# Attention then two gated products on one core: where float64 weight conversion starts, in buffers of its own, and the order of the first transfers

## The chip, the cores and the metric

The kernel runs on one core of a Trainium2 chip, with 32-bit float data at full accuracy. The metric is device time in microseconds (us) of one execution; lower is better. TensorE (PE) multiplies matrices, VectorE (DVE), ScalarE (ACT) and GpSimd (POOL) work on tiles, SyncE (SP) issues nearly all transfers. Each engine runs its own instructions strictly in the order in which they stand, so an instruction that waits holds everything behind it.

## The reference

```
h = phi(q), phi(k):  phi(x) = exp(x@omega.T - |x|^2/2 - max) / sqrt(128), x scaled by 64**-0.25
attn = (phi(q) @ (phi(k).T @ v)) / (phi(q) @ sum(phi(k)) + 1e-6)    # 4 batches, 8 heads, 576 x 64
x  = attn as 2304 tokens x 512
g  = silu(x @ w_in);                      x = g @ w_out       # 512 -> 2048 -> 512
g  = silu(x @ w_gate) * (x @ w_val);      out = g @ w_out2    # 512 -> 1536 -> 512
```

The weights reach the chip as float64 words (512 x 2048 and 512 x 1536, and back) and are turned into float32 there.

## The kernel before

**Stages.** Attention runs 72 steps of 128 tokens (8 units of two batch-and-head pairs, 9 steps each). Then follow up 1 (products with w_in), down 1 (w_out), up 2 (w_gate, w_val) and down 2 (w_out2). Every matrix product is done by Strassen's scheme with seven products of half size (numbered 1 to 7, in the order 1, 5, 6, 2, 7, 3, 4 for the down stages), and every float32 operand is split into a rounded high part (made by ACT or POOL) and a low part (the rest, made by DVE or POOL); a product takes high x high, high x low and low x high, so three matmuls.

**Attention.** `load_piece` brings 384 columns of k or q, `split_piece` splits them, `proj` multiplies them by omega (`om_hi`, `om_lo`), `soft` takes the row maximum on DVE (`reduce_max`, L805) and the exponentials on ACT (L809), `kv_tr` and `num` form the sums, `recip`, `spread`, `finish` and `store` divide and write x to DRAM (`x_d`). Working tiles come from `f_work`: nine places in the big tile `fa` and one tile `extra`. Steps are written out in fixed order.

**Up 1.** 24 groups `n` of seven products (8 weight blocks by 3 token ranges s, 384 + 384 tokens each); the first three blocks run over s = 0, then 1, then 2. `x_prep` loads and splits x for one s (into tiles `ra`, `rb`, `rc` for s = 0, 1, 2). After each group four results go to DRAM (`g_d`), 96 in all. Copies between accumulator banks are ACT's (L1160), sums DVE's (L1217), silu ACT's (L1184).

**Conversion.** `conv_job` turns one block of float64 words into float32: two loads (512 KB each), per half a Prelu on ACT (L343), a shift (L350) and an or (L357) on DVE, four sums on POOL (L376), then either a split for up 1 (`conv_job("in", i)`) or three stores of 0.9 MB for a later stage (`down_job`). Blocks in 0, 1, 2 and down 0 are converted during attention, the rest (list `jobs`) in up 1. They use `f_raw` (two load buffers at R_AT), `f_c` and `f_sum`.

**What sets the order.** For the later stages a planner writes instructions as it walks through the products: each operation has an engine, an estimated cost and the keys it needs; `flush` emits what its clocks say is ready, from `urgent` and the streams z, wd, split, x, conv. The down stage's weight loads (stream wd, L1315, split at L1319 and L1323), its first inputs (stream z, L1341, only when the conv stream is empty) and their splits (L1367 on ACT, L1371 and the Strassen sums L1391 on DVE) share the queues with up 1.

**Where conversion starts in up 1.** x for s = 1 is loaded partly into the raw buffers' place (`xr1`), and six places of conversion's buffers are lent to `f_s` (result tiles). So `hook1` starts the conversion only when that x is split and all lent places are back:

```python
def hook1(n, p):
    if conv_may and len(f_s.gone) == len(lent):
        conv_may.clear()
        streams["conv"].extend(conv1)
```

Of the kernel before, what the change touches and what calls it, by code (L numbers as in the profile page):

```python
# [9 lines left out]
F32 = mybir.dt.float32  # L10
# [32 lines left out]
def kernel(  # L43
# [21 lines left out]
    UB = 2  # L65
# [46 lines left out]
    class Free:  # L112
        def __init__(self, name, items):
            self.name = name
            self.q = deque((x, 0.0) for x in items)
            self.retire, self.gone = [], []

        def close(self, some):

            self.retire = some  # L120
            self.gone += [x for x, _ in self.q if any(x is y for y in some)]
            self.q = deque(y for y in self.q if not any(y[0] is z for z in some))
# [534 lines left out]
    def xr1(j, c):  # L657
        return cut(fa, (XR_AT, R_AT)[j] + c * N, N)
# [44 lines left out]
    f_work.give(vp.tile([P, S], F32, name="extra"), 0.0)  # L703
# [12 lines left out]
    CW = UT // 3  # L716

# [13 lines left out]
    def load_v(u):  # L731
        v = v_t[u % 2]
        half = NCH // 2
        for b in range(UB):
            B, p = u_of(u, b)
            for h in range(2):
# [4 lines left out]
                nc.sync.dma_start(out=v[:, c0 : c0 + half, o : o + D], in_=whole)  # L741
                part = src[:D] if b else src[half * P :]
                nc.sync.dma_start(out=v[b * D : (b + 1) * D, half, o : o + D], in_=part)
# [14 lines left out]
    nc.vector.memset(om, 0.0)  # L758
    for h in range(2):
        nc.sync.dma_start(out=om[h * D : (h + 1) * D, h * M : (h + 1) * M], in_=omT)  # L760
    warm = const.tile([P, 1], F32, name="warm")
    nc.gpsimd.memset(warm, 0.0)
    nc.scalar.activation(warm, warm, AF.Exp)
    for i in range(3):
        for nm in ("k", "q"):
            load_piece(0, nm, i)
# [3 lines left out]
    load_v(0)  # L770
# [170 lines left out]
    later, left_over, lent = {}, [], []  # L941
# [4 lines left out]
    for nm, i in pieces:  # L946
        split_piece(0, nm, i)
    for nm, i in pieces:
        load_piece(1, nm, i)
# [4 lines left out]
    def step(s):  # L954
# [34 lines left out]
        if s < NSTEP:  # L989
            if u + 1 < NU and c == LAG:  # L990
                load_v(u + 1)
# [37 lines left out]
    def end_attention():  # L1029
# [12 lines left out]
        lent.extend(cut(fa, o + i * N, N) for o, n in ((C_AT + S // 3, 3), (SUM_AT, 2), (R_AT + 4 * N, 1)) for i in range(n))  # L1042
        for x in lent:
            f_s.give(x, 0.0)

        def rest(ub, n):
# [10 lines left out]
            def after_store(end):  # L1057
                T["xd", B, p] = end + 0.5
                waits.remove(ub)
                if ub[0] == NU - 2 and not any(u == NU - 2 for u, _ in waits):  # L1060
                    f_c.give(c_slot, end)
                    f_s.close(lent)
                    while shut:
                        f_s.give(shut.pop(), end)
# [471 lines left out]
    def up_order(kinds, n, head, tail):  # L1536
# [8 lines left out]
        lambda: x_prep(0, 1, xr1, False, "DVE", then=lambda t: conv_may.append(t)),  # L1545
# [9 lines left out]
    opened, conv_may = [], []  # L1555
# [31 lines left out]

    def hook1(n, p):
        if conv_may and len(f_s.gone) == len(lent):
            conv_may.clear()  # L1590
# [124 lines left out]
```

## Time and profile before

| | |
|---|---|
| three runs | 943.35, 946.96, 947.23 us; median 946.96 |
| the profiled execution | 950.47 us, span 948.7 us |
| busy share of the span | PE 96%, DVE 70%, ACT 60%, POOL 23% |
| stages | attention to about 168 us, up 1 to 352, down 1 to 541, up 2 to 809, down 2 to the end |

A row of a timeline gives the start, the duration, engine, line, operation, output and input, and in brackets how long the engine was idle before it and what ended that. Rows of SPq are the issue of transfers, not the transfers.

### The profile page before, as it was taken

Reading aid. Unit: us, or ns where it says so; the run is one execution under the profiler, and the core shown is the slowest. Engines: PE = TensorE matmul, PEld = TensorE weight load, DVE = VectorE, ACT = ScalarE, POOL = GpSimd, SP = SyncE. Lnnn points to the kernel's source line nnn. Section 1 sums busy time; section 2 is a strip of 40 time slices with the busy share of each in tenths; the row PEclk is TensorE's granted clock in tenths of the full one; section 3 lists DMA queues with packets and bytes.
Section 4 is the critical chain, followed back from the end, with each engine's and each line's share of the span. In section 5 each row is a group of like instructions: output and inputs, shape, how many; then the busy total and the mean of one; then the engine's idle time right before and its main releaser. Section 6 shows DMA issues by size and latency. Waiting matters only on the chain.

```text
span 948.7 us, 15565 instructions
## 1 busy us (share of the span) xinstructions
PE 909.3 (96%) x5313; PEld 883.0 (93%) x5313; DVE 660.6 (70%) x1041; ACT 567.9 (60%) x1231; POOL 214.0 (23%) x258
## 2 busy tenths in 40 slices
PE   7888889999999998999999899999999999899998
PEld 7877778899999997999999799999999999899998
DVE  4667778778575459678589889765647456968594
ACT  6766777677666775545446685544545437545453
POOL 6566885013444200000000012421212110000000
PEclk9989999999999998999999999999999999999999
DMA  6756763688989995551731556643535249472701
GB/s 172 188 159 177 222 178 85 190 274 281 306 288 309 336 392 216 159 175 50 232 119 56 196 165 200 214 157 131 171 112 176 75 138 334 134 207 69 238 20 67
DMA packets 129856, 174.80 MB, mean 184 GB/s; under 512 B 34288, under 2 KB 111728, under 8 KB 129776
## 3 DMA queue, kind: packets, MB, share of 16 engines
q1 hardware_dynamic: 129776, 173.80, 57.6%
q8 instruction: 42, 0.69, 0.3%
q14 instruction: 38, 0.31, 0.1%
HBM read 111.74 MB, written 61.94 MB: 183 GB/s over the span
## 4 chain that ended last, share of the span: by engine, by line
PE 77%; DMA 8%; DVE 6%; ACT 5%; issue 2%; SPq 1%; POOL 0%; DVEq 0%; ACTq 0%
PE ps L1143 39%; PE ps L1508 29%; PE ps L881 2%; ACT kq L809 2%; DMA g_d<-fa 2%; PE ps L829 2%; DMA dn<-fa 2%; DVE nb L805 1%; PE ps L795 1%; PE ps L796 1%; PE ps L797 1%; PE ps L843 1%; DMA fa<-x_d 1%; DMA rc<-wd_out 1%; DMA fa<-g_d 1%
## 5 line engine op out<-in xcount | busy, mean ns | idle before, releaser
L376 POOL TENSOR_TENSOR fa<-fa 128x256 f32<-128x256 f32 x136 | 113.2, 845 | 505.0 <-DVE fa L357 276.9
L1143 PE MATMUL ps<-ra 128*128 128x384 f32 x840 | 156.0, 335 | 3.5 <-ACT ps L1160 3.5
L1143 PE MATMUL ps<-rb,ra 128*128 128x384 f32 x840 | 157.5, 340 | 0.7 <-ACT ps L1160 0.7
L1143 PE MATMUL ps<-rc,ra 128*128 128x384 f32 x840 | 156.6, 339 | 0.1
L1143 PEld LDWEIGHTS ps<-ra 128*128 128x128 f32 x840 | 146.7, 188 | 5.1 <-ACT ps L1160 5.1
L1143 PEld LDWEIGHTS ps<-rb,ra 128*128 128x128 f32 x840 | 148.6, 188 | 1.6 <-ACT ps L1160 1.6
L1143 PEld LDWEIGHTS ps<-rc,ra 128*128 128x128 f32 x840 | 148.3, 188 | 0.4 <-ACT ps L1160 0.4
L1371 DVE TENSOR_TENSOR ra<-fa,ra 128x768 fp32r<-128x768 f32 x105 | 100.5, 957 | 51.9 <-PE ps L1508 30.5
L1367 ACT ACTIVATE ra<-fa 128x768 fp32r<-128x768 f32 x105 | 88.0, 845 | 81.2 <-PE ps L1508 69.2
L1160 ACT ACTIVATE ps<-ps 128x384 f32<-128x384 f32 x180 | 85.3, 475 | 82.6 <-PE ps L1143 77.9
L1217 DVE TENSOR_TENSOR fa<-fa,ps 128x384 f32<-128x384 f32 x120 | 66.2, 552 | 92.4 <-ACT ps L1160 71.5
L1508 PE MATMUL ps<-ra,rb 128*128 128x384 f32 x720 | 129.2, 340 | 0.0
L1508 PEld LDWEIGHTS ps<-ra,rb 128*128 128x128 f32 x720 | 127.9, 189 | 0.5 <-DVE ra L1371 0.3
L1508 PE MATMUL ps<-ra 128*128 128x384 f32 x612 | 110.8, 339 | 6.9 <-DVE ra L1371 6.7
L1508 PEld LDWEIGHTS ps<-ra 128*128 128x128 f32 x612 | 107.3, 190 | 9.4 <-DVE ra L1371 8.5
L809 ACT ACTIVATE kq<-ps,nb 128x128 f32<-128x128 f32 x288 | 82.2, 381 | 40.5 <-DVE nb L805 40.3
L1508 PE MATMUL ps<-ra,rc 128*128 128x384 f32 x432 | 78.5, 340 | 2.5 <-DVE ra L1371 2.5
L1508 PEld LDWEIGHTS ps<-ra,rc 128*128 128x128 f32 x432 | 76.0, 188 | 4.1 <-DVE ra L1371 3.9
L1391 DVE TENSOR_TENSOR fa<-ra,fa 128x768 f32<-128x768 f32 x63 | 60.1, 954 | 1.4 <-DMA ra<-g_d 0.7
L805 DVE TENSOR_REDUCE nb<-ps 128x4 f32<-128x512 f32 x72 | 49.0, 684 | 16.6 <-PE ps L797 11.6
L1184 ACT ACTIVATE fa<-fa 128x384 f32<-128x384 f32 x84 | 43.8, 521 | 27.1 <-DVE fa L1217 26.8
L829 PE MATMUL ps<-v,kq 128*128 128x65 f32 (+1 forms) x320 | 44.8, 279 | 12.8 <-ACT kq L809 8.4
(100 smaller groups left out, 1232.0 us busy)
## 6 DMA issues: line engine op xcount, KB each, us to landing
g_d<-fa SPq DMA_DIRECT2D x168, 192.0 KB, 3.7
fa<-g_d SPq DMA_DIRECT2D x42, 384.0 KB, 4.3
ra<-g_d SPq DMA_DIRECT2D x42, 384.0 KB, 4.0
fa<-in_moe_w_out SPq DMA_DIRECT2D x28, 512.0 KB, 5.2
fa<-in_moe_w_in SPq DMA_DIRECT2D x16, 512.0 KB, 5.4
wd_out<-fa SPq DMA_DIRECT2D x14, 512.0 KB, 3.3
fa<-in_moe_w_gate SPq DMA_DIRECT2D x12, 512.0 KB, 3.8
fa<-in_moe_w_val SPq DMA_DIRECT2D x12, 512.0 KB, 5.6
```

The lines of the kernel that those rows point to most:

```text
L376: f(blk(f"S{n}"), blk(l), blk(r))
L805: nc.vector.reduce_max(nb, ps.rearrange("p i (h m) -> p (i h) m", h=2), axis=AX.X, negate=True)
L809: nc.scalar.activation(e[:, i, h * M : (h + 1) * M], ps[:, i, h * M : (h + 1) * M], AF.Exp, bias=nb[:, 2 * i + h : 2 * i + h + 1],)
L829: nc.tensor.matmul(acc[:, o : o + VH], e[a:z, 0, h * M : (h + 1) * M], vs[u][a:z, c, o : o + VH], start=first and h == 0, stop=last, skip_ ...
L1143: nc.tensor.matmul(ps[b][:, :N], cut(l, j * P, P), cut(r, j * N, N), start=start and c == 0, stop=stop and c == 5, skip_group_check=True,)
L1160: nc.scalar.activation(out() if callable(out) else out, src, AF.Copy)
L1184: nc.scalar.activation(b["t"], src, AF.Silu)
L1217: nc.vector.tensor_add(t, t if in_place else p5[n], ps[bank_][:, :N])
L1367: nc.scalar.activation(ops[s, p, k][0], src(), AF.Copy)
L1371: nc.vector.tensor_sub(l, src(), h.bitcast(F32))
L1391: (nc.gpsimd if eng == "POOL" else nc.vector).tensor_sub(z(PLACE[to]), z(PLACE.get(l, l)), z(PLACE.get(r, r)))
L1508: nc.tensor.matmul(ps[BANKS[p] + e][:, :N], cut(a, e * P, P), b, start=p in FIRST and i == 0 and c == 0, stop=p in LAST and i == fp - 1 an ...
```

## The change

Four edits belong together. (1) x for s = 1 gets a tile of its own (`xr1_t`) beside the v tiles; attention gets four extra working tiles in place of one, and unit NU-2 takes them first, so that conversion's third buffer (`c_slot`) is free when attention's loop ends; nothing is lent. (2) `hook1` starts the conversion stream at n = 0, product 1 (`CONV_P`). (3) `jobs` has down 1 and down 2 first, then in i and down i. (4) The start of attention: k's first piece is loaded before omega, q's first after it, the first half of v on ACT's queue, the other pieces and the rest of v later; only the first pieces are split ahead of the loop; omega is scaled and split on DVE alone; seven matmuls of zeros stand first on PE.

```diff
-        return cut(fa, (XR_AT, R_AT)[j] + c * N, N)
+        return cut(xr1_t, c * N, N) if j else xr(j, c)
...
+        if u == NU - 2:
+            f_work.q = deque(sorted(f_work.q, key=lambda y: any(y[0] is w for w in works)))
...
-    f_work.give(vp.tile([P, S], F32, name="extra"), 0.0)
+    for i in range(4):
+        f_work.give(vp.tile([P, S], F32, name=f"extra{i}"), 0.0)
+    xr1_t = vp.tile([P, 4 * N], F32, name="xr1")
...
-    nc.vector.memset(om, 0.0)
+    zero = const.tile([P, M], F32, name="zero")
+    nc.vector.memset(zero, 0.0)
+    load_piece(0, "k", 0)
     for h in range(2):
         nc.sync.dma_start(out=om[h * D : (h + 1) * D, h * M : (h + 1) * M], in_=omT)
+    load_piece(0, "q", 0)
+    load_v(0, 0, nc.scalar)
...
-    for i in range(3):
+    for i in range(1, 3):
         for nm in ("k", "q"):
             load_piece(0, nm, i)
-    load_v(0)
+    load_v(0, 1)
+    for i in range(WARM):
+        nc.tensor.matmul(ps[0][:, :M], zero, zero, start=True, stop=True)
...
-    nc.vector.tensor_scalar_mul(om, om, SCALE)
-    nc.scalar.activation(om_hi, om, AF.Copy)
-    nc.vector.tensor_sub(om_lo, om, om_hi.bitcast(F32))
+    nc.vector.tensor_scalar_mul(om_hi, om, SCALE)
+    nc.vector.scalar_tensor_tensor(om_lo, om, SCALE, om_hi.bitcast(F32), op0=ALU.mult, op1=ALU.subtract)
...
-    for nm, i in pieces:
-        split_piece(0, nm, i)
-    for nm, i in pieces:
-        load_piece(1, nm, i)
+    for nm in ("k", "q"):
+        split_piece(0, nm, 0)
...
+        if 0 <= s < 2:
+            for nm in ("k", "q"):
+                split_piece(0, nm, s + 1)
+        if s == 1:
+            for nm, i in pieces:
+                load_piece(1, nm, i)
...
-        lent.extend(cut(fa, o + i * N, N) for o, n in ((C_AT + S // 3, 3), (SUM_AT, 2), (R_AT + 4 * N, 1)) for i in range(n))
-        for x in lent:
-            f_s.give(x, 0.0)
+        assert all(o + S <= C_AT for o in taken)
+        f_c.give(c_slot, 0.0)
...
-    jobs = [down_job(0, 1)]
+    jobs = [down_job(0, 1), down_job(0, 2)]
     for i in range(3, FP[0]):
-        jobs += [conv_job("in", i)] + [down_job(0, i - 1)]
-    jobs.append(down_job(0, FP[0] - 1))
+        jobs += [conv_job("in", i), down_job(0, i)]
...
-        if conv_may and len(f_s.gone) == len(lent):
-            conv_may.clear()
+        if n == 0 and p == CONV_P:
             streams["conv"].extend(conv1)
```

PE's row of instructions is the same in both but for the seven matmuls of zeros. Three places where the others change follow; line numbers differ by a few between the two files.

DVE at the start of attention, before (om is cut from `fa`; lok and loq are low parts of k and q, nb the maxima of a step):

```order
L758 MEMSET fa 128x256
L768 MEMSET v_98 128x9
L769 MEMSET v_98 128x9
L768 MEMSET v_99 128x9
L769 MEMSET v_99 128x9
L782 TENSOR_SCALAR fa<-fa 128x256
L784 TENSOR_TENSOR om_lo<-fa,om_hi 128x256
L753 TENSOR_TENSOR lok<-rawk,hik 128x384
L753 TENSOR_TENSOR loq<-rawq,hiq 128x384
L753 TENSOR_TENSOR lok<-rawk,hik 128x384
L753 TENSOR_TENSOR loq<-rawq,hiq 128x384
L805 TENSOR_REDUCE nb<-ps_78 128x4
```

and now:

```order
L754 MEMSET zero 128x128
L761 MEMSET fa 64x128 x2
L766 MEMSET v_102 128x9
L767 MEMSET v_102 128x9
L766 MEMSET v_103 128x9
L767 MEMSET v_103 128x9
L785 TENSOR_SCALAR om_hi<-fa 128x256
L786 SCALAR_TENSOR_TENSOR om_lo<-fa,om_hi 128x256
L748 TENSOR_TENSOR lok<-rawk,hik 128x384
L748 TENSOR_TENSOR loq<-rawq,hiq 128x384
L807 TENSOR_REDUCE nb<-ps_78 128x4
L748 TENSOR_TENSOR lok<-rawk,hik 128x384
```

The first step's maximum has moved ahead of the second pieces' low parts, and omega's split no longer passes through ACT.

ACT at the start of up 1, before (L1160 copies a bank, L578 makes the high part of x for s = 1 in `rb`):

```order
L1102 ACT_TABLE_LOAD
L1102 ACTIVATE silu<-silu 128x1
L578 ACTIVATE rb<-fa 128x384 x2
L1160 ACTIVATE ps_83<-ps_80 128x384
L1160 ACTIVATE fa<-ps_82 128x384
L1184 ACTIVATE fa<-ps_78 128x384
```

and now (L333 is conversion's Prelu, L568 the high part, `xr_93` the new tile):

```order
L1106 ACT_TABLE_LOAD
L1106 ACTIVATE silu<-silu 128x1
L333 ACTIVATE fa<-fa 128x512
L1164 ACTIVATE ps_83<-ps_80 128x384
L1164 ACTIVATE fa<-ps_82 128x384
L333 ACTIVATE fa<-fa 128x512
L568 ACTIVATE rb<-fa 128x384
L1188 ACTIVATE fa<-ps_78 128x384
L568 ACTIVATE rb<-xr_93 128x384
```

What stood ahead of the first bank copy waited for x; what stands there now waits for a weight block.

DVE at the end of up 1, before (L1217 a result sum, L1323 the low part of down 1's weights, L1371 that of its inputs, L1391 a Strassen sum):

```order
L1371 TENSOR_TENSOR ra<-fa,ra 128x768
L1217 TENSOR_TENSOR fa<-fa,ps_80 128x384
L1391 TENSOR_TENSOR fa<-fa 128x768
L1217 TENSOR_TENSOR fa<-fa,ps_83 128x384
L1371 TENSOR_TENSOR ra<-fa,ra 128x768
L1391 TENSOR_TENSOR fa<-fa 128x768
L1323 TENSOR_TENSOR rb<-rb 128x768
L1323 TENSOR_TENSOR rb<-rb 128x512
L1217 TENSOR_TENSOR fa<-fa,ps_81 128x384
L1323 TENSOR_TENSOR rb<-rb 128x768
L1217 TENSOR_TENSOR fa<-fa,ps_83 128x384
L1323 TENSOR_TENSOR rb<-rb 128x768
```

and now, from up 1's last result sum on (L1221; L1327 weights, L1375 inputs, L1395 sums):

```order
L1221 TENSOR_TENSOR fa<-fa,ps_83 128x384
L1327 TENSOR_TENSOR rb<-rb 128x768
L1375 TENSOR_TENSOR ra<-fa,ra 128x768
L1395 TENSOR_TENSOR fa<-fa 128x768
L1375 TENSOR_TENSOR ra<-fa,ra 128x768
L1395 TENSOR_TENSOR fa<-fa 128x768
L1375 TENSOR_TENSOR ra<-fa,ra 128x768
L1395 TENSOR_TENSOR fa<-fa 128x768
L1327 TENSOR_TENSOR rc<-rc 128x512
L1375 TENSOR_TENSOR ra<-fa,ra 128x768
L1327 TENSOR_TENSOR rc<-rc 128x768 x2
L1395 TENSOR_TENSOR fa<-fa 128x768
```

Six of the seven weight parts in `rb` now stand ahead of the last result sum instead of three; no input split stands ahead of it any more, where there were two pairs.

## Rows read from the trace of the kernel before

**Rows 1.** The page, busy us (share of the span) and instructions of each engine.
```profile
PE 909.3 (96%) x5313; PEld 883.0 (93%) x5313; DVE 660.6 (70%) x1041; ACT 567.9 (60%) x1231; POOL 214.0 (23%) x258
```

**Rows 2.** Table by stretch: length, busy per engine, granted clock, DMA share, GB/s; up 2.
```profile
610.00:780.00 170.00, 170.00 (x970) 170.00 (x969) 93.81 (x176) 81.54 (x172) 33.17 (x43) 1.00 0.40 135
```

**Rows 3.** Timeline of the start: start us, us, engine, line, operation.
```profile
0.86 0.27 DVE L758 MEMSET fa<- 128x256 f32 x1 [0.86 <-PEq L1704]
...
1.16 1.21 SPq L760 DMA_DIRECT2D fa<-in_omega  x2
...
4.11 0.29 DVE L782 TENSOR_SCALAR fa<-fa 128x256 f32<-128x256 f32 x1 [2.90 <-DMA fa<-in_omega]
...
5.73 0.58 PE L795 MATMUL ps<-om_hi,hik 128*128 128x256 f32 x1 [5.73 <-POOL hik L751]
...
8.60 0.56 DVE L753 TENSOR_TENSOR loq<-rawq,hiq 128x384 fp32r<-128x384 f32 x1 [0.40 <-POOL hiq L751]
...
9.07 1.28 DVE L805 TENSOR_REDUCE nb<-ps 128x4 f32<-128x512 f32 x2
...
9.38 0.41 PE L796 MATMUL ps<-om_hi,lok 128*128 128x256 f32 x1
...
9.79 3.20 ACT L809 ACTIVATE kq<-ps,nb 128x128 f32<-128x128 f32 x12 [4.94 <-DVE nb L805]
...
12.17 0.28 PE L796 MATMUL ps<-om_hi,loq 128*128 128x256 f32 x1
...
13.39 1.14 ACT L809 ACTIVATE kq<-ps,nb 128x128 f32<-128x128 f32 x4 [0.40 <-DVE nb L805]
```

**Rows 4.** Table by stretch, columns as in rows 2, while the first pieces land.
```profile
6.00:8.00 2.00, 1.99 (x7) 1.44 (x8) 1.19 (x3) 0.00 (x0) 1.52 (x3) 1.00 0.91 249
```

**Rows 5.** Chain that ended last, start us and us: a weight block's load in attention.
```profile
76.37 4.06 DMA fa<-in_moe_w_out
```

**Rows 6.** Timelines of SP, ACT and PE where up 1 begins.
```profile
168.24 4.77 SPq L899 DMA_DIRECT2D dn<-v  x4
173.10 3.85 SPq L549 DMA_DIRECT2D fa<-x_d  x8
...
175.70 1.01 ACT L578 ACTIVATE rb<-fa 128x384 fp32r<-128x384 f32 x2 [2.25 <-DMA fa<-x_d]
176.62 0.47 ACT L1160 ACTIVATE ps<-ps 128x384 f32<-128x384 f32 x1
...
199.42 0.68 ACT L343 ACTIVATE fa<-fa 128x512 f32<-128x512 f32 x1
...
177.15 14.83 PE L1143 MATMUL ps<-ra 128*128 128x384 f32 x84 [1.41 <-ACT ps L1160]
```

**Rows 7.** Timelines of DVE, PE, SP, ACT where down 1 begins, and one stretch.
```profile
342.51 0.96 DVE L1371 TENSOR_TENSOR ra<-fa,ra 128x768 fp32r<-128x768 f32 x1 [4.94 <-ACT ra L1367]
...
351.65 0.55 DVE L1217 TENSOR_TENSOR fa<-fa,ps 128x384 f32<-128x384 f32 x1
...
372.20 3.02 DVE L1323 TENSOR_TENSOR rc<-rc 128x512 fp32r<-128x512 f32 x4
375.14 0.95 DVE L1391 TENSOR_TENSOR fa<-ra,fa 128x768 f32<-128x768 f32 x1
376.01 0.95 DVE L1371 TENSOR_TENSOR ra<-fa,ra 128x768 fp32r<-128x768 f32 x1
...
351.82 4.50 PE L1508 MATMUL ps<-ra 128*128 128x384 f32 x25
...
377.01 1.97 PE L1508 MATMUL ps<-ra 128*128 128x384 f32 x5 [1.40 <-DVE ra L1371]
...
359.03 4.85 SPq L1315 DMA_DIRECT2D rc<-wd_out  x7
...
366.84 0.63 ACT L1319 ACTIVATE rc<-rc 128x512 fp32r<-128x512 f32 x1 [3.11 <-DMA rc<-wd_out]
...
376.00:378.00 2.00, 0.99 (x3) 0.99 (x4) 2.00 (x4) 0.00 (x0) 0.00 (x0) 0.50 0.00 0
```

More of the change, by code (lines that the diff above doesn't have):

```diff
@@ L115, in __init__ @@
             self.q = deque((x, 0.0) for x in items)
[L116 to L122, printed above, removed]
         def take(self):
@@ L716 @@
     CW = UT // 3
+    WARM = 7
     def runs(lo, hi):
@@ L729, in load_piece, with load_v @@
             nc.sync.dma_start(out=t[:, a:z], in_=src[p * P : (p + 1) * P, t0 : t0 + z - a])
-    def load_v(u):
+    def load_v(u, b, eng=nc.sync):
         v = v_t[u % 2]
         half = NCH // 2
-        for b in range(UB):
+        for b in (b,):
             B, p = u_of(u, b)
@@ L740, in load_v @@
                 c0 = b * (half + 1)
-                nc.sync.dma_start(out=v[:, c0 : c0 + half, o : o + D], in_=whole)
+                eng.dma_start(out=v[:, c0 : c0 + half, o : o + D], in_=whole)
                 part = src[:D] if b else src[half * P :]
-                nc.sync.dma_start(out=v[b * D : (b + 1) * D, half, o : o + D], in_=part)
+                eng.dma_start(out=v[b * D : (b + 1) * D, half, o : o + D], in_=part)
         vs[u] = v
@@ L757 @@
     om = cut(fa, SUM_AT, 2 * M)
-    nc.vector.memset(om, 0.0)
+    zero = const.tile([P, M], F32, name="zero")
+    nc.vector.memset(zero, 0.0)
+    load_piece(0, "k", 0)
     for h in range(2):
         nc.sync.dma_start(out=om[h * D : (h + 1) * D, h * M : (h + 1) * M], in_=omT)
+    load_piece(0, "q", 0)
+    load_v(0, 0, nc.scalar)
+    for h in range(2):
+        nc.vector.memset(om[h * D : (h + 1) * D, (1 - h) * M : (2 - h) * M], 0.0)
     warm = const.tile([P, 1], F32, name="warm")
@@ L964, in step @@
             soft(s)
+        if 0 <= s < 2:
+            for nm in ("k", "q"):
+                split_piece(0, nm, s + 1)
+        if s == 1:
+            for nm, i in pieces:
+                load_piece(1, nm, i)
         for f in then:
@@ L990, in step @@
             if u + 1 < NU and c == LAG:
-                load_v(u + 1)
+                load_v(u + 1, 0)
+                load_v(u + 1, 1)
             if c in PIECES:
@@ L1060, in after_store @@
                 if ub[0] == NU - 2 and not any(u == NU - 2 for u, _ in waits):
-                    f_c.give(c_slot, end)
-                    f_s.close(lent)
                     while shut:
@@ L1544 @@
     to_come += [
-        lambda: x_prep(0, 1, xr1, False, "DVE", then=lambda t: conv_may.append(t)),
+        lambda: x_prep(0, 1, xr1, False, "DVE"),
         lambda: x_prep(0, 2, xr2, False, "DVE", before=1, then=xr2_end),
     ]
-    jobs = [down_job(0, 1)]
+    jobs = [down_job(0, 1), down_job(0, 2)]
     for i in range(3, FP[0]):
-        jobs += [conv_job("in", i)] + [down_job(0, i - 1)]
-    jobs.append(down_job(0, FP[0] - 1))
+        jobs += [conv_job("in", i), down_job(0, i)]
     jobs += [up_job_dram("gate"), up_job_dram("val")]
     conv1 = weave(*jobs)
-    opened, conv_may = [], []
+    opened = []
     extra_c, extra_raw = cut(fa, XR_AT, 512), cut(fa, XR_AT + 512, 1024)
```

9 lines of the change are left out of this document (3 added, 6 removed).

## The prediction

> **What bounds the kernel.** I read the busy line first: PE is busy 96% of the span [rows 1], so only time in which PE waits or runs slowly can be won. The table by stretch then says where that is. In up 2, 970 matmuls fill 170 us without a gap, 0.175 us each [rows 2]. Attention has waits of its own on DVE and on small transfers, and the joints between stages have some; of these the change touches three places: attention's first 10 us, the first products of up 1, the first products of down 1. In PE's own timeline the first matmul starts at 5.73 us and the first exponential at 9.79 [rows 3]; at up 1's start PE idles 1.41 us for a bank copy [rows 6]; at down 1's start it begins at 351.82 and by 377.01 has done only p1, p5 and the first group of p6 [rows 7]. That is nine groups of 12 matmuls, 18.9 us of work at 0.175 us, in 25.2 us: 6.3 us are lost, and the clock is at 0.50 (the lower level, 1.2 GHz) in 376 to 378 [rows 7] after these waits: 5 matmuls take 1.97 us from 377.01 where 0.9 would do. I put the whole slow piece at 1.5 us.
>
> **Part 1, the start of attention.** Omega's first transfer waited for a memset that ended at 1.13 and went out at 1.16, 0.6 us per issue [rows 3]. Now k's piece goes first at about 0.8 and omega's two follow at 1.4 and 2.0, where the second went out at 1.78: omega lands about 0.2 us later, near 4.3. Its chain loses the hop to ACT and back: om_hi is ready on DVE at 4.3 + 0.29 = 4.6 [rows 3], om_lo near 5.0 (0.4 us, by the 0.56 of a split of 384 columns). k's high part no longer ends the wait, so PE starts near 4.7 instead of 5.73, and q's parts come 0.5 to 0.6 us earlier. The first maximum, which stood behind the second pieces' low parts (the last at 8.60 + 0.56) and ran at 9.07, now stands ahead of them and can run near 7.0, and the first exponentials near 7.7 instead of 9.79. That 2.1 us does not all stay: the second maximum still stands behind the same low part, so it ends near 9.8, and ACT then has three steps of 1.07 us in a row (3.20 for 12 instructions [rows 3]): the fourth step's exponentials start near 12.0 instead of 13.39. So 1.4 us, of which I count **1.2**. Bounds: 2.1 above; below, a loss of 1.2, if v's first half (288 KB, now issued on ACT's queue from the very start) holds up omega and k by its own bytes at the 249 GB/s of 6 to 8 us [rows 4].
>
> The seven matmuls of zeros fill PE from about 1.1 us until omega is there (four issues of v stand on ACT, whose first work is at 7.7, and cost nothing there). Before, a matmul of 256 columns takes 0.41 us at 9.38 and 0.28 at 12.17 [rows 3], after PE had been busy since 5.73. If the zeros bring that step forward, the second and third step's products are shorter; behind the low part of 9.16 this moves nothing, so I count 0 for it (between 0 and 0.3).
>
> Here a rule speaks against the edit. The Trainium skill, "DMA: Bandwidth & Descriptors", section "Issuing engines are not separate DMA queues", says that transfers started by different engines run on the same 16 DMA engines and interleave, and that a second issuing engine saves only issue time. The DMA share of 0.91 at 6 to 8 us [rows 4] agrees that these engines are nearly full there; no run here shows two issuing queues at once. By the rule the start would be worth nothing or less, 943.6 or more; that is the second rival below.
>
> The rest of attention keeps its instructions and their order on PE; three more working tiles change names, not waits. I carry the 1.2 us through, with 1 us either way for transfers that meet differently.
>
> **Part 2, the start of up 1.** The bank copy at 176.62 stood behind the high part of x, which waited until 175.70 for a transfer issued at 173.10 [rows 6]. In its place stands now a Prelu on weights whose load goes out between dn's second and third issue, near 169.7. A weight load in attention took 4.06 us [rows 5], so it lands near 173.8; with 0.68 us for the Prelu, as at 199.42 [rows 6], the copy is done by 175.0, before PE needs it at 177.15 - 1.41 = 175.74. The wait goes: **1.3** of 1.41. What is late next is the high part of x, now behind 1 MB of weights; its first product is 14 products of 1.05 us later, so that is covered. Two Prelus, two shifts and an or now stand between ACT's and DVE's work for up 1: about 3 us, by the Prelu's 0.68, over 35 us in which both have gaps. Bounds: 1.41 above; if the load takes as long as the 7.81 us from 359.03 to 366.84 [rows 7], the copy ends at 178.7, 1.6 us later than now: a loss of 1.6. I stay near the first, since at 170 us little else is moving.
>
> **Part 3, from up 1 to down 1.** One down block more is converted early, and SP's order shows what is left of it: by 28 of the 96 result stores both kernels have issued the same loads of w_in, and the conversion's end is ahead by 2 to 4 stores of 1.9 us each. The gap at 352 to 377 is DVE's: it must finish every row up to the low part for the second group of p6 (376.01). Counted in the new order from the last result sum (351.65 + 0.55 = 352.2 [rows 7]): 19 splits and sums at 0.87 us (375.14 to 376.01), five weight parts of 768 columns at 0.87, three of 512 at 0.6 (four mixed ones take 3.02) make 16.5 + 4.4 + 1.8 = 22.7 us, so 374.9 if nothing waits. Before, two pairs of splits were done by 347 (the first at 342.51), but more weight parts were left, and the first weight part of `rc` waited until 366.84. Now none of the input splits is done when up 1 ends, so PE waits some 2 us at 352 that it did not wait before; that lies inside the same DVE row and is not added. The loads of `rc` go out near 353 instead of 359.03, with two input loads ahead of them instead of eight, and should land near 357.5 to 358, when DVE comes to them; I allow 0.6 us of waiting: 375.5 against 377.01, 1.5 us. PE's waits are then shorter and spread, and I give the slow clock behind them 0.6 us of its 1.5 back. **2.1** in all. Bounds: 1.5 + 1.6 + 1.5 = 4.0 or so if nothing waits, the clock stays up and p6's groups close up; below, a loss of 1.5 (first rival).
>
> **The sum.** 1.2 + 1.3 + 2.1 = 4.6 us. Against the profiled execution, 950.47 - 4.6 = 945.9; that one is 3.5 us above the median of the runs, so against 946.96 I expect **942.4**.
>
> **Rivals.** *`rc` stands in the way* (15%): its first low part is now the eighth row after the last sum, ahead of p1's fourth low part. If that load takes 7.81 us as now, it lands at 360.8 and DVE loses 3 us there: 378.5, 1.5 later than 377.01. Then 946.96 - 1.2 - 1.3 + 1.5 = 946.0. For it: the DMA engines were full here; against: fewer bytes ahead. *v crowds out the first pieces* (7%): its 288 KB, on the move from 0.8 us on, come between omega and the pieces of k and q; 1.2 us at 249 GB/s, so the start gives nothing or loses 1.2, and the time is 943.6 to 944.8. Against it: no transfer is issued before 1.16 as it is [rows 3], so there is room ahead. *Everything opens* (25%): 2.1, 1.4 and 4.0 make 7.5, so 939.5; it needs the clock to stay at full after 352, which it did not after waits of the same length. *Slower* (8%): x for s = 2. Its first loads now stand after result store 11 instead of 9, and its high parts four ACT rows later, behind more conversion. Its first product is 36 products after the one at 177.15, near 215; store 11 comes of group 2, near 195, and a load of some 4 us [rows 5] leaves about 15 us for 28 splits on ACT and DVE. It decides from there: if loads and rows together come over 15 us later than that, every product with this x waits in turn. Ten us lost against 4.6 won is 952.4. The middle of the conversion not moving at all is in the first rival.
>
> **How the numbers follow.** The forecast has 45%, half of it on each side of 0.5% (4.7 us, about what a measurement can tell from no change). Faster: 25 + 22 = 47%; slower 8%; the rest, 45%, is within 0.5%. The range leaves out the slower case and the tip of the fast one: 938.0 to 948.5. The likeliest case alone runs from 940.5 to 945.
>
> **What would show it.** Right: first exponential near 7.7 and the fourth step's near 12; no PE wait of over 0.5 us from 170 to 180; PE's second group of p6 near 375.5 minus 2.5 us of shift, with a new wait of about 2 us where down 1 starts. Wrong: exponentials still near 9.8; ACT's first Prelu in up 1 after 175; the first `rc` low part after 360; any PE wait over 1 us between 190 and 230.

## The result, and the profile of the changed kernel

| | median of the runs | ratio to before (95% interval) |
|---|---|---|
| before (10 runs) | 947.29 us | |
| after (10 runs) | 952.08 us | 1.0052 (1.0036 to 1.0069) |
| predicted | 942.4 us (938.0 to 948.5) | faster 47%, within 0.5% 45%, slower 8% |

The change costs 4.8 us. The two profiled executions differ by less, 952.04 against 950.47 us, because the profiled execution of before lay 3 us over its median; sizes below come from the medians, places from the profiles.

The busy line of the page of after hardly differs from [rows 1]; PE shows 3.0 us more, and the seven matmuls of zeros alone take 3.4 (1.05 to 4.41 us). So most of what is lost does not show as busy time; PE's own timeline shows it as waits. A row gives the start, the duration, engine, line, operation and, in brackets, the idle time ahead of it and what ended that:

```profile
PE 912.3 (96%) x5327; PEld 884.9 (93%) x5327; DVE 660.5 (70%) x1043; ACT 566.4 (60%) x1230; POOL 216.2 (23%) x258
...
166.83 1.20 PE L1147 MATMUL ps<-ra 128*128 128x384 f32 x6
...
170.44 17.85 PE L1147 MATMUL ps<-ra 128*128 128x384 f32 x102
188.70 1.34 PE L1147 MATMUL ps<-ra 128*128 128x384 f32 x6 [0.41 <-ACT ps L1164]
...
192.99 1.33 PE L1147 MATMUL ps<-ra 128*128 128x384 f32 x6 [0.84 <-ACT ps L1164]
...
214.64 1.31 PE L1147 MATMUL ps<-rb,ra 128*128 128x384 f32 x6 [2.11 <-ACT ps L1164]
...
300.37 4.44 PE L1147 MATMUL ps<-ra 128*128 128x384 f32 x24 [0.57 <-ACT ps L1164]
...
345.72 9.20 PE L1147 MATMUL ps<-rc,ra 128*128 128x384 f32 x42 [1.77 <-ACT ps L1164]
...
356.05 0.44 PE L1512 MATMUL ps<-ra 128*128 128x384 f32 x1 [0.95 <-ACT ra L1371]
...
379.71 3.24 PE L1512 MATMUL ps<-ra 128*128 128x384 f32 x17 [1.72 <-DVE ra L1375]
```

Up 1's first product starts at 166.83; in before the same row reads

```profile
168.83 1.21 PE L1143 MATMUL ps<-ra 128*128 128x384 f32 x6
```

so after leads by 2.0 us there, and by more when the 1.41 us of [rows 6] do not come: 102 matmuls run from 170.44 without a gap. From then on the lead is spent: these five waits for bank copies (L1164) are 5.7 us, where before had two, of 0.33 and 0.69 us, behind the 1.41. Behind the last of them PE also runs slowly: 42 matmuls take 9.20 us from 345.72, where 0.175 us each would make 7.4, and the granted clock there (row of the table by stretch, columns as in [rows 2]) is at the lower level, 1.2 GHz:

```profile
347.00:350.00 3.00, 3.00 (x12) 3.00 (x11) 1.34 (x2) 2.59 (x6) 0.00 (x0) 0.50 1.01 364
```

Down 1 begins at 356.05 instead of 351.82 and its second group of p6 at 379.71 instead of 377.01 [rows 7].

ACT's timeline shows what stood ahead of the two long ones. First the wait at 214.64:

```profile
208.26 0.51 ACT L1188 ACTIVATE fa<-fa 128x384 f32<-128x384 f32 x1
211.94 0.66 ACT L333 ACTIVATE fa<-fa 128x512 f32<-128x512 f32 x1 [3.17 <-DMA wd_out<-fa]
...
214.11 0.48 ACT L1164 ACTIVATE ps<-ps 128x384 f32<-128x384 f32 x1
```

The second Prelu of in 3 stands 3.17 us for its target buffer, which down 2's block still fills: its three stores, issued from 205.81 on, have not landed. The bank copy that PE needs is the fifth row behind it. Then the wait at 345.72:

```profile
337.13 0.32 SPq L1319 DMA_DIRECT2D rb<-wd_out  x1
...
339.82 0.49 ACT L1164 ACTIVATE fa<-ps 128x384 f32<-128x384 f32 x1 [0.56 <-DMA fa<-g_d]
344.06 0.84 ACT L1323 ACTIVATE rb<-rb 128x768 fp32r<-128x768 f32 x1 [3.75 <-DMA rb<-wd_out]
344.81 0.47 ACT L1188 ACTIVATE fa<-ps 128x384 f32<-128x384 f32 x1
345.18 0.48 ACT L1164 ACTIVATE ps<-ps 128x384 f32<-128x384 f32 x1
```

The first weight part for `rb` waits 3.75 us for a load issued at 337.13 that needs 6.9 us. In before the same part stood behind two input splits and four more results of up 1, and ACT did not wait for it, though its load, issued at 338.54, was no faster:

```profile
346.30 0.85 ACT L1319 ACTIVATE rb<-rb 128x768 fp32r<-128x768 f32 x1
```

### The profile page after: what moved, and what is told of

It is laid out like the page before. It is cut to its first block, busy times and chain, and to the rows that moved or that the text cites. A ratio compares the mean times of both kernels' runs of the same rounds, so it can differ in the third digit from the quotient of the medians.

```text
span 950.2 us, 15577 instructions
## 1 busy us (share of the span) xinstructions
PE 912.3 (96%) x5327; PEld 884.9 (93%) x5327; DVE 660.5 (70%) x1043; ACT 566.4 (60%) x1230; POOL 216.2 (23%) x258
## 4 chain that ended last, share of the span: by engine, by line
PE 69%; DMA 10%; DVE 9%; ACT 7%; issue 4%; SPq 1%; DVEq 0%; ACTq 0%
PE ps L1147 34%; PE ps L1512 29%; ACT kq L811 2%; DVE nb L807 1%; PE ps L831 1%; PE ps L883 1%; DMA fa<-in_moe_w_out 1%; DMA wd_out<-fa 1%; DVE ra L409 1%; PE ps L798 1%; DMA fa<-in_moe_w_in 1%; PE ps L797 1%; PE ps L799 1%; DVE fa L347 1%; DVE fa L1221 1%
## 5 line engine op out<-in xcount | busy, mean ns | idle before, releaser
L1371 ACT ACTIVATE ra<-fa 128x768 fp32r<-128x768 f32 x105 | 88.1, 844 | 81.7 <-PE ps L1512 63.5
L1164 ACT ACTIVATE ps<-ps 128x384 f32<-128x384 f32 x180 | 85.4, 475 | 84.9 <-PE ps L1147 79.9
L1375 DVE TENSOR_TENSOR ra<-fa,ra 128x768 fp32r<-128x768 f32 x105 | 100.5, 957 | 44.9 <-PE ps L1512 32.6
L1221 DVE TENSOR_TENSOR fa<-fa,ps 128x384 f32<-128x384 f32 x120 | 66.1, 551 | 91.1 <-ACT ps L1164 65.2
L1395 DVE TENSOR_TENSOR fa<-ra,fa 128x768 f32<-128x768 f32 x63 | 60.1, 954 | 0.9 <-DMA ra<-g_d 0.3
```

The lines of the kernel that those rows point to most:

```text
L1164: nc.scalar.activation(out() if callable(out) else out, src, AF.Copy)
L1221: nc.vector.tensor_add(t, t if in_place else p5[n], ps[bank_][:, :N])
L1371: nc.scalar.activation(ops[s, p, k][0], src(), AF.Copy)
L1375: nc.vector.tensor_sub(l, src(), h.bitcast(F32))
L1395: (nc.gpsimd if eng == "POOL" else nc.vector).tensor_sub(z(PLACE[to]), z(PLACE.get(l, l)), z(PLACE.get(r, r)))
```

## Experiments

"Old order" is `down 1, in 3, down 2, in 4, down 3, ...`, "new order" is that of the change, `down 1, down 2, in 3, down 3, in 4, ...`.

| run | what it is | median us | ratio to before (95%) |
|---|---|---|---|
| e1 | before + edit 4 (start of attention) | 945.47 | 0.9983 (0.9965 to 1.0001) |
| e2 | after without edit 4 | 953.79 | 1.0060 (1.0038 to 1.0082) |
| e3 | after, old order of blocks | 944.82 | 0.9986 (0.9967 to 1.0004) |
| e4 | e3, conversion begun at group 3 | 945.02 | 0.9975 (0.9962 to 0.9988) |
| e5 | after, all weight loads planned 7 us later | 956.57 | 1.0111 (1.0090 to 1.0131) |
| e6 | after, in 3 ahead of down 2 | 956.28 | 1.0092 (1.0069 to 1.0115) |
| e7 | after, old order from in 4 on | 948.40 | 1.0020 (1.0002 to 1.0038) |
| e8 | e1, v's first half last | 944.89 | 0.9981 (0.9968 to 0.9995) |
| e9 | after, first `rb` load planned 6 us later | 950.15 | 1.0025 (1.0010 to 1.0040) |
| e10 | e7, down 2's buffers planned 6 us later | 948.28 | 1.0012 (0.9996 to 1.0028) |
| e11 | after, both estimates changed | 945.20 | 0.9981 (0.9965 to 0.9998) |
| e12 | old order, conversion begun in two parts, v in between | 946.77 | 0.9993 (0.9977 to 1.0009) |
| e13 | e8 without the zeros | 947.36 | 1.0003 (0.9989 to 1.0017) |
| e14 | before + later splits alone | 947.09 | 1.0004 (0.9986 to 1.0021) |
| e15 | e4 + v's first half last | 945.75 | 0.9990 (0.9972 to 1.0007) |
| e16 | before + zeros alone | 945.83 | 0.9992 (0.9978 to 1.0007) |
| e17 | e4 + v in between | 944.97 | 0.9980 (0.9963 to 0.9996) |

The intervals are 0.0013 to 0.0023 either way, so a difference between two runs is known to about 2 us. Differences below are of medians; by the ratios some come out up to 1 us otherwise.

### The start of attention, or the conversion

> The kernel before with edit 4 alone (order of the first transfers, omega split on DVE, zeros on PE); conversion, buffers and blocks as before. Theory A (what costs is in up 1, the start gains): up 1's first product about 2 us earlier, as in the pair of profiles (166.83 against 168.83), and nothing lost behind it: 945.3, ratio 0.998. Theory B (the new start costs, the rest is neutral): 951 to 952, ratio 1.004 or more. If the 2 us of the pair were the clock in attention and not the edit: 947, ratio 1.000.

> The kernel after with the start of attention as it was (edits 1 to 3 without edit 4). Theory A: the start's gain goes and the loss in up 1 stays, 953 to 954, ratio 1.007. Theory B: 947, ratio 1.000. In the profile, by A, PE waits of 0.8 to 2 us between 190 and 220 and near 345, as in the kernel after.

Theory A holds: edit 4 alone gives 1.7 us (its interval just includes none), edits 1 to 3 alone cost 6.6 us, and the two make 4.9 against 4.8 measured for the whole. All that is lost is lost with the conversion.

### The early start, or the order of the blocks

```diff
-    jobs = [down_job(0, 1), down_job(0, 2)]
+    jobs = [down_job(0, 1)]
     for i in range(3, FP[0]):
-        jobs += [conv_job("in", i), down_job(0, i)]
+        jobs += [conv_job("in", i)] + [down_job(0, i - 1)]
+    jobs.append(down_job(0, FP[0] - 1))
```

> The kernel after with the blocks in the old order (down 1, then in i and down i - 1), the early start and all else kept. From the 30th result store on SP's loads then stand as in the kernel before. Theory A1 (the early start itself costs): waits between 185 and 220 stay, up 1 from 300 on is as before: the lead of 0.5 us that the kernel after has left at 223 stays, 946.8, ratio 0.9995. Theory A2 (the order of the blocks costs, through the end of up 1, where weight parts wait ahead of bank copies): no wait of over 1 us near 345, and the lead of 2.8 us at up 1's start stays at least in half: 944.5 to 946, ratio 0.997 to 0.9985. If neither: 952, as the kernel after.

e4 has, besides, `if n == 3 and p == CONV_P`.

> The kernel after with the old order of blocks and conversion begun at group 3 instead of group 0: the buffers of their own and the new start of attention are what is left. Theory A: as the start alone, 945.3, ratio 0.998, with the wait of about 1.4 us at up 1's start back and none over 1 us from 190 to 220. If the buffers themselves cost (more working tiles, another sequence of places): above 948.

A2: with the old order the early start costs nothing and the loss of 7.3 us (952.1 against 944.8; 6.3 by the ratios) is gone. Nor does the early start gain: with it 944.8, without it 945.0 (where one wait of 1.21 us, at 209.46, is over the 1 us that was expected at most). PE's timeline of e3 shows why:

```profile
169.56 17.85 PE L1147 MATMUL ps<-ra 128*128 128x384 f32 x102
188.85 1.32 PE L1147 MATMUL ps<-ra 128*128 128x384 f32 x6 [1.45 <-ACT ps L1164]
...
193.30 1.33 PE L1147 MATMUL ps<-ra 128*128 128x384 f32 x6 [1.04 <-ACT ps L1164]
...
198.01 15.87 PE L1147 MATMUL ps<-rb,ra 128*128 128x384 f32 x90 [0.20 <-ACT ps L1164]
213.72 1.20 PE L1147 MATMUL ps<-rc,ra 128*128 128x384 f32 x6
```

The 1.41 us saved where up 1 begins come back as 1.45 and 1.04 us at 188.85 and 193.30; but there is no wait at 214. What held the first of these copies is a result sum on DVE, which stood until the store of an earlier result had ended:

```profile
185.71 0.55 DVE L1221 TENSOR_TENSOR fa<-fa,ps 128x384 f32<-128x384 f32 x1 [3.28 <-DMA g_d<-fa]
...
186.29 0.53 ACT L1188 ACTIVATE fa<-fa 128x384 f32<-128x384 f32 x1 [2.32 <-DVE fa L1221]
...
188.32 0.47 ACT L1164 ACTIVATE ps<-ps 128x384 f32<-128x384 f32 x1
```

After has this wait too (2.95 us at 185.56); e4, which differs from e3 only in the group at which conversion begins, has none there. On SP the first result store goes out at 182.35 in e3 and at 178.21 in e4: in e3 the next weight load (178.47) and two loads of attention's last rows are issued ahead of it.

The table by stretch (length, busy time and count of each engine, granted clock, DMA share, GB/s) for 210 to 220 us, e3 first, then after:

```profile
210.00:220.00 10.00, 10.00 (x60) 10.00 (x59) 7.65 (x15) 8.47 (x21) 0.00 (x0) 1.00 0.53 189
```

```profile
210.00:220.00 10.00, 7.89 (x46) 7.57 (x45) 6.60 (x11) 7.06 (x17) 3.43 (x4) 1.00 0.92 314
```

A block of w_out brings three stores to DRAM, a block of w_in none. With two w_out blocks in a row, the second's stores fall into 205 to 212 us, right behind the loads of x for s = 2, and the DMA engines stay full.

### The front of up 1, or its end

```diff
 e6    jobs = [down_job(0, 1), conv_job("in", 3), down_job(0, 2), down_job(0, 3)]
       for i in range(4, FP[0]):
           jobs += [conv_job("in", i), down_job(0, i)]
 e7    jobs = [down_job(0, 1), down_job(0, 2), conv_job("in", 3)]
       for i in range(4, FP[0]):
           jobs += [conv_job("in", i)] + [down_job(0, i - 1)]
       jobs.append(down_job(0, FP[0] - 1))
```

> The kernel after with in 3 ahead of down 2 again, and from down 3 on the new order (down 1, in 3, down 2, down 3, in 4, down 4, ...). The front is that of the kernel with the old order, the end (first weight part in rb behind result 88) that of the kernel after. Theory E: the wait near 346 stays, and 948.5 to 950.5 is left, ratio 1.002 to 1.0035. Theory F: the loss goes, 945 to 946.

> The complement: down 1, down 2, in 3, then the old cadence (in 4, down 3, in 5, down 4, ...). The front is that of the kernel after; at the end one input split stands ahead of the first weight part in rb, which stands behind result 89. Theory E: the 2.11 us at 214.64 stay, the wait near 346 is gone or under 1 us: 947 to 949. Theory F: 950 to 952.

e7 came out as theory E says: the wait at the front is there (2.23 us at 213.75), none near 346, and 3.6 us are left over e3, so the other 3.7 (952.1 against 948.4) go with the end of the order. Each half is known to about 2 us, and the 3.6 need not all lie at the front (next section). e6 missed its forecast: it lost its wait near 214 and kept one at the end (1.26 us at 351.21), but it puts w_in's last block so late that PE waits for its weights, and that alone is worse than what was to be measured:

```profile
301.90 9.22 PE L1147 MATMUL ps<-ra 128*128 128x384 f32 x40 [5.45 <-DVE ra L409]
```

### Taking the two waits away, the order kept

The planner decides where a part stands by its estimate of when its data are there. e5 and e9 change the estimate of weight loads, e10 and e11 that of the return of down 2's buffers:

```diff
 e5, e9, e11   (all loads + 7.0; the first load into rb + 6.0; + 8.0)
+        def then(end):
+            T[key("r")] = end + late
 e10, e11
-                    done(clk["end"] + 2.0)
+                    done(clk["end"] + (8.0 if (kind, i) == ("out", 2) else 2.0))
```

> The kernel after in all but one estimate: the planner is told that down 1's weight loads land 7 us later. The first weight part in rb then stands on ACT behind result 92 of 96 as in the kernel before (88 in the kernel after), and two input splits stand ahead of it. Theory E (of what the new order of blocks costs, most is lost at the end of up 1, where a weight part that waits for its load holds a bank copy: ACT idle 3.75 us, PE 1.77 us, results 84 to 95 fall back by 3.8 us): that wait goes, 948.3, ratio 1.001. Theory F (it is lost at the front, where conversion of w_in waits for the stores of two blocks of w_out: PE 2.11 us at 214.64): unchanged, 951 to 952.

> The kernel after, with one estimate changed: the planner is told that the first load into rb (weights for p6 of down 1) lands 6 us later. Up to there every engine's row is as in the kernel after; on ACT the first weight part in rb now stands behind result 92 instead of 88 and two input splits ahead of it, as in the kernel before. By the end half of the loss (3.7 us, 952.1 against 948.4 of the kernel whose end is the old one): no ACT wait of 3.75 us near 340, no PE wait of over 0.3 us between 340 and 350, down 1 starts as in that kernel, 948.5, ratio 1.002. If weight parts held back only move the wait into down 1 (as the PE wait of 4.06 us at 368.5 in the kernel with all weight loads 7 us late hints): 951 to 953.

e5 took the wait near 346 away, and down 1 then waits for its own operands (4.06 us, below). But its edit also moved the loads of up 2 and down 2, and that is where its loss over after lies: from up 2's first product to the end e5 takes 415.0 us (540.14 to 955.13) and after 407.6 (542.67 to 950.23). So its time settles nothing.

```profile
368.50 10.90 PE L1515 MATMUL ps<-ra 128*128 128x384 f32 x53 [4.06 <-DVE ra L1378]
```

e9 moves one place alone. ACT's timeline has the two input splits at 342.29 and the weight part at 347.49, neither waiting, and PE runs from 331.30 to down 1's first product at 352.28 without a gap:

```profile
331.30 20.96 PE L1147 MATMUL ps<-rc,ra 128*128 128x384 f32 x120
...
352.28 4.50 PE L1518 MATMUL ps<-ra 128*128 128x384 f32 x25
357.37 4.26 PE L1518 MATMUL ps<-ra 128*128 128x384 f32 x23 [0.59 <-DVE ra L1381]
...
364.99 10.18 PE L1518 MATMUL ps<-ra 128*128 128x384 f32 x48 [2.43 <-DVE ra L1381]
```

It gains 1.9 us over after (2.6 by the ratios) where 3.7 were expected. A wait of 2.43 us stands at 364.99 in down 1, but all of PE's waits from down 1's first product up to 379.7 are 5.0 us in e9 and 4.9 in after, so that the gain was lost there isn't shown.

> The kernel with down 1, down 2, in 3 and then the old cadence, with one estimate changed: the planner is told that down 2's buffers come back 6 us later. The second Prelu of in 3, which waited 3.17 us for these stores on ACT, then stands some 11 rows later. If that Prelu is the front half of the loss: no ACT wait of over 1 us between 205 and 215, PE's wait near 214 under 0.5 us instead of 2.2, and 945.0 to 946 instead of 948.4. If the transfers there are the cause, whatever stands on ACT: PE waits elsewhere before 225 and 948 stays.

> The kernel after, all edits and its own order of blocks, with both estimates changed (down 2's buffers 6 us later, first load into rb 8 us later, which puts its part behind result 92). If these two waits are what the order of blocks costs: both PE waits gone and 945 to 946, ratio 0.998 to 0.999, as with the old order. If one is only moved: 948 to 949.

e11 wins all of it back: 945.2, the time of the old order. e10 missed its forecast: with the Prelu moved it should have come to 945 to 946 and stayed at 948.3. Its ACT, like that of e11 below, shows that the front is not quite free: the row no longer waits for the Prelu's buffer but for result tiles that are still on their way to DRAM.

```profile
215.40 0.49 ACT L1164 ACTIVATE fa<-ps 128x384 f32<-128x384 f32 x1 [1.06 <-DMA g_d<-fa]
...
217.82 0.49 ACT L1188 ACTIVATE fa<-ps 128x384 f32<-128x384 f32 x1 [1.52 <-DMA g_d<-fa]
```

PE's wait there is 1.52 us in e10 and 1.00 in e11, against 1.67 to 2.23 in the five profiles with two blocks of w_out in a row and the old estimate (after, e2, e5, e7, e9). The DMA share there is 1.00 in e10 (212 to 222 us) and 0.98 in e11 (210 to 220), no emptier than in after. So at the front it is both ACT's order and the traffic that cost. The rest of the difference between e10 and e11 lies behind up 1, where PE waits 0.46 + 0.55 + 2.42 + 1.71 = 5.1 us at down 1's start in e10 and 0.16 + 1.65 + 1.56 = 3.4 in e11. The starts of up 1's first product, of down 1's first product and of the first matmul that reads `rb` there, and the lengths between them, put six profiles side by side:

| | up 1's first | down 1's first | down 1's first with `rb` | up 1, us | down 1's start, us |
|---|---|---|---|---|---|
| e3 | 165.94 | 349.00 | 374.08 | 183.1 | 25.1 |
| after | 166.83 | 356.05 | 382.79 | 189.2 | 26.7 |
| e7 | 165.01 | 351.26 | 379.12 | 186.3 | 27.9 |
| e9 | 165.51 | 352.28 | 379.74 | 186.8 | 27.5 |
| e10 | 170.57 | 354.07 | 382.75 | 183.5 | 28.7 |
| e11 | 168.67 | 352.75 | 378.36 | 184.1 | 25.6 |

In e10 up 1 is as short as in e3: moving the Prelu did free up 1, and what e10 has left over e3 lies where down 1 starts. e7 is long in both places. So in these profiles the loss from the order of blocks has a third place, down 1's start, and the halves of e7 are not a split by place. Each is a single profile, with stretches at the lower clock in it. That the two estimates together carry the loss is shown by e11; why e11's down 1 starts better than that of e9 isn't settled.

### What edit 4 does in attention

> The kernel before with edit 4, but v's first half goes last on SP's queue instead of first on ACT's. If v's 288 KB are what made omega land 1.1 us later in the kernel after (its split began at 5.23 instead of 4.11): omega's split begins near 4.3, the first product with omega near 4.7 instead of 5.7, the first exponentials near 8.0 instead of 9.0, time 944.5. If k's piece ahead of omega is the cause: still 5.2, 5.7 and 9.0, and the time that of edit 4 alone, 945.5.

The first rows of after, then of e8, answer to [rows 3]:

```profile
0.73 0.47 ACTq L736 DMA_DIRECT2D v<-in_v  x1
...
5.23 0.29 DVE L785 TENSOR_SCALAR om_hi<-fa 128x256 fp32r<-128x256 f32 x1 [3.68 <-DMA fa<-in_omega]
...
9.01 1.14 ACT L811 ACTIVATE kq<-ps,nb 128x128 f32<-128x128 f32 x4 [4.28 <-DVE nb L807]
...
13.77 1.15 ACT L811 ACTIVATE kq<-ps,nb 128x128 f32<-128x128 f32 x4 [0.75 <-DVE nb L807]
```

```profile
4.00 0.29 DVE L791 TENSOR_SCALAR om_hi<-fa 128x256 fp32r<-128x256 f32 x1 [2.45 <-DMA fa<-in_omega]
...
7.86 1.15 ACT L817 ACTIVATE kq<-ps,nb 128x128 f32<-128x128 f32 x4 [5.63 <-DVE nb L813]
...
13.32 1.14 ACT L817 ACTIVATE kq<-ps,nb 128x128 f32<-128x128 f32 x4 [1.74 <-DVE nb L813]
```

e8 issues v's first half behind all pieces, on SP's queue:

```diff
-    load_v(0, 0, nc.scalar)
...
+    load_v(0, 0)
     load_v(0, 1)
```

v's bytes on ACT's queue hold omega up by 1.2 us, though omega's two loads go out from 1.18 us on in both: its split begins at 4.84 to 5.59 us in the ten profiles with v on ACT's queue and at 3.94 to 4.11 in the nine without. With v last, omega and the first exponentials come when the prediction said (4.6 for om_hi, 7.7), but the fourth step's still at 13.3: PE stood idle for 1.25 us before the sums with v (row below), and the step's products stand behind these. The profile names the exponentials as what ended that wait, but those of the first step were done at 9.0 us; the last of v's loads went out at 9.92. In time e8 is no different from e1.

```profile
11.16 0.41 PE L837 MATMUL ps<-v,kq 128*128 128x65 f32 x2 [1.25 <-ACT kq L817]
```

e13 is e8 with `WARM = 0`; e14 has of edit 4 only the two hunks on `split_piece` and `load_piece(1, ...)`; e16 has of it only `zero`, its memset and the seven matmuls.

> Edit 4 on the kernel before with v's first half last on SP's queue, as in the earlier run, but without the seven matmuls of zeros. Theory Z (the zeros are what edit 4 gives): back to 946.5 to 947, ratio 0.9995 to 1.000. Theory S (it is the later splits and loads of the pieces, or the transfers): 944.9 to 945.5, ratio 0.998 to 0.9985, as with the zeros.

> The kernel before with one piece of edit 4: the second and third pieces are split in steps 0 and 1, and the pieces of the next unit are loaded at step 1, instead of all ahead of the loop; omega, the first transfers and v as before, no zeros. If the place of these splits and loads is what edit 4 gives: 945 to 945.5, ratio 0.998 to 0.9985. If it is the order of the first transfers: 947, ratio 1.000.

> The kernel before with only the seven matmuls of zeros put first on PE (and their memset first on DVE). If the zeros are what edit 4 gives (0.9981 with them, 1.0003 without): 945 to 945.5, ratio 0.998 to 0.9985, and matmuls of 256 columns fall from 0.41 to 0.28 us earlier than at 11.7. If the zeros only make up for the pauses that the new order puts between PE's first products (full rate at 14.8 without them): 946.8, ratio 1.000.

Without the zeros the gain is gone; the later splits alone give none; the zeros alone stand in between, and their interval holds both none and the whole. In the profile of e13 a matmul of 256 columns takes 0.41 us until 14.6 us and 0.28 after it; in that of e8 it is at 0.28 from 11.74, in before from 11.8:

```profile
14.60 0.40 PE L804 MATMUL ps<-om_hi,loq 128*128 128x256 f32 x1
14.81 0.30 PE L805 MATMUL ps<-om_lo,hiq 128*128 128x256 f32 x1
...
15.69 0.28 PE L804 MATMUL ps<-om_hi,lok 128*128 128x256 f32 x1
```

That fits the loss of the gain, but it is one profile of each, and this moment scatters between executions (last section): it is 9.37 in e16, but 9.93 in e14, which has no zeros. That the zeros are the cause isn't shown.

### Versions meant to beat both kernels

e12 and e17 issue v's first half on SP's queue between the second and third pieces; e12 also converts down 1 from group 0 and the rest from group 3; e15 is e4 with v last, as in e8.

```diff
 e12, e17
     for i in range(1, 3):
         for nm in ("k", "q"):
             load_piece(0, nm, i)
+        if i == 1:
+            load_v(0, 0)
 e12
         if n == 0 and p == CONV_P:
-            streams["conv"].extend(conv1)
+            streams["conv"].extend(weave(down_job(0, 1)))
+        if n == 3 and p == CONV_P:
+            streams["conv"].extend(conv1)
```

> A version meant to beat both: old order of blocks, down 1's conversion begun at group 0 and the rest at group 3, and v's first half on SP's queue between the second and third pieces. The wait of 1.42 us at up 1's start should stay away (Prelu ahead of the first bank copy instead of x), and with in 3 loaded later the two waits at 188.9 and 193.3 (1.45 and 1.04 us with the early start) should shrink to under 1 us together: 943.5 to 944.5, ratio 0.9965. If the two waits come from x for s = 1 and its rows, not from in 3: 945.

> A version meant to beat both: buffers of their own, old order of blocks, conversion begun at group 3 (the best so far, ratio 0.9975), and v's first half last on SP's queue, which brought the first exponentials to 7.9 us. If the two add up: 944.3, ratio 0.997; if the start's order is all the same behind the first 13 us: 944.8, ratio 0.9975.

> Buffers of their own, old order of blocks, conversion begun at group 3 (measured 945.0, ratio 0.9975), and v's first half on SP's queue between the second and third pieces: in the run that had this start the fourth step's exponentials began near 11.6 instead of 13.7 and matmuls reached 0.28 us at 8.9. If time won in the first 12 us is carried to the end: 943.3, ratio 0.996. If it is lost again in attention's later waits: 945, ratio 0.9975, though the fourth step starts near 11.6.

e12 missed its forecast: 946.77 is no faster than before. The wait at up 1's start stays away, but 0.51 and 1.10 us remain at 186.74 and 191.29 although in 3 now loads later, and 0.61 and 1.39 us come at 206.95 and 212.85, the second behind a Prelu that waited 2.45 us for its load. e15 adds nothing to e4. e17's exponentials of the fourth step start earlier than in e4 (13.66) and e15 (12.54), which have the same base:

```profile
11.83 1.15 ACT L812 ACTIVATE kq<-ps,nb 128x128 f32<-128x128 f32 x4 [0.25 <-DVE nb L808]
```

That is 1.8 us ahead of e4 and what the prediction forecast for after (12.0), yet e17 takes 944.97 where e4 takes 945.02. Time won in the first 12 us is not seen at the end; with the two intervals a part of it may be there all the same. e1, e3, e4, e8, e11 and e17 beat after by some 0.7%; against before e4, e8, e11 and e17 are 0.2% faster with intervals that leave 1 out, and no one of them can be told from the others.

## Why the prediction failed, by its own steps

**What bounds the kernel** held: what moved the time is waits of PE and, behind some of them, stretches at the lower clock.

**Part 1, the start (forecast -1.2, measured -1.7 with e1).** The size is right by luck, for the steps are not. Omega was to land 0.2 us later; it landed 1.1 us later (5.23 against 4.11), since v did crowd it out, the mechanism of the second rival, though not its price, for the start did gain. The rule of the Trainium skill quoted there ("DMA: Bandwidth & Descriptors", section "Issuing engines are not separate DMA queues": transfers of different issuing engines interleave on the same DMA engines) describes it; this case now shows it with 5.23 against the 4.00 of e8. The fourth step came at 13.77, not near 12.0, and so later than the 13.39 of before: the gain can't have come by that path. The zeros were counted as nothing; in e13 the edit without them gives nothing (1.0003). And the carry, all of a gain at 12 us to the end, is not borne out by e17. Where edit 4's 1.7 us arise stays open.

**Part 2, the start of up 1 (forecast -1.3).** The wait went as forecast: the first Prelu ran at 171.86, ahead of the copy at 172.43. The step that failed is the carry from there: the text asked only whether some 3 us of conversion work on ACT and DVE fit into 35 us with gaps, and put what follows at nothing. 0.41 and 0.84 us came back at 188.70 and 192.99 (1.45 and 1.04 in e3). The first was held by a result sum that waited 2.95 us on DVE (3.28 in e3) for the store of a result, a term that the prediction does not have: the early loads stand ahead of up 1's first result stores on SP. Ahead of the second copy stood a part of x that waited for DVE (1.10 us at 190.87 in e3) and a Prelu that waited 0.43 us for its buffer; e12, which has no Prelu there, still waits 1.10 us. Net of e3 and e4: nothing.

**Part 3, up 1 to down 1 (forecast -2.1; the order of blocks measured +7.3, by the ratios +6.3).** This term sank the forecast. It read the new order of blocks as conversion "ahead by 2 to 4 stores" and looked at its effect in one place, DVE's row at the joint. What it left out is what the order does while up 1 runs: where w_out's stores fall (PE's wait of 2.11 us at the front) and where down 1's weight parts are put among up 1's bank copies (1.77 us at the end and the slow stretch behind it). With both placed otherwise the loss is gone (e11). At the joint itself even the counted part was mis-sized. From the last result sum to the end of the low part that p6 waits for DVE took 379.65 - 355.31 = 24.3 us, against 376.96 - 352.20 = 24.8 in [rows 7] and 23.3 forecast (22.7 and 0.6 of waiting). The count itself was off: 17 splits and sums stand in this stretch, not 19, so by the prediction's own costs the work is 21.0 us; the waits are 0.91, 1.01 and 0.28 us, 2.2 where 0.6 was allowed. The weight part in `rc` ran at 363.31, 7.1 us after its load went out, where 4.5 to 5 were counted. That is past the 360 that the text named as wrong, and it is the first rival's condition, but DVE lost 1.01 us there and not 3. Nor did the clock give its 0.6 us back: it is at 0.57 in 357 to 361 us of after, behind waits of 0.95 and 0.68 us.

```profile
354.76 0.55 DVE L1221 TENSOR_TENSOR fa<-fa,ps 128x384 f32<-128x384 f32 x1
...
378.70 0.95 DVE L1375 TENSOR_TENSOR ra<-fa,ra 128x768 fp32r<-128x768 f32 x1
...
356.23 1.28 SPq L1319 DMA_DIRECT2D rc<-wd_out  x3
...
363.31 0.63 ACT L1323 ACTIVATE rc<-rc 128x512 fp32r<-128x512 f32 x1 [5.06 <-DMA rc<-wd_out]
```

**The rivals.** "Slower" named the right stretch (195 to 230, behind more conversion) and its sign, "any PE wait over 1 us between 190 and 230" did appear, 2.11 us. But it made x for s = 2 the culprit and asked for a delay of 15 us before anything is lost; the row that held was a bank copy, and a few rows behind a waiting Prelu were enough. That its 952.4 is near the measured time is luck. The wait at the end of up 1 was no rival at all, though the order showed six of seven `rb` parts moved ahead of the last result sum; this was noted for DVE and not followed to ACT, which makes the high parts.

## What to carry to other kernels

Where a planner writes the order, an edit to one list moves every later instruction: walk each in-order engine through the whole stretch and ask of each row that waits for a transfer which bank copy stands behind it, and of each new load which result store stands behind it on the issuing queue, not only at the place the edit aims at. Cost a block that stores to DRAM by the stretch in which its stores run and how full the DMA engines already are there. Before a gain early in a stage is carried to the end, ask what else sets the next meeting point: here 1.8 us won at 12 us were not found at the end.

## What the chip showed that was not expected

PE's first matmuls are slow for a stretch whose end moves between executions of the same instructions. e3 and after share the whole start of attention; the first product of 0.28 us runs at 9.67 in e3 and at 12.42 in after, and the exponentials of the fourth step follow it (12.77 and 13.77). Over the ten profiles that share this start it lies between 9.6 (e7) and 13.0 us (e10).

Stretches at the lower clock fall differently in attention in each profile: the mean granted clock is 0.68 in 60 to 70 us in before, so partly at the lower level (1.2 GHz), and 0.66 in 40 to 50 in after, which is at full speed in 60 to 70. A single profile carries several such stretches, so a lead of 2 us at attention's end in one pair of profiles is no measure of an edit:

```profile
60.00:70.00 10.00, 9.52 (x51) 8.52 (x52) 8.39 (x18) 8.68 (x29) 3.01 (x3) 0.68 0.57 154
```

```profile
40.00:50.00 10.00, 7.01 (x32) 6.16 (x31) 4.70 (x11) 6.70 (x23) 7.17 (x8) 0.66 0.69 182
```
